# One tile shape for both matmul groups of an attention kernel: 64 rows by 32 columns, with two buffers of scores and two banks of sums

## The chip, the core and the metric

The kernel runs on one core of a Trainium2 chip. A core has five engines that each follow their own instruction queue: TensorE (PE in the profile, with its weight loads shown apart as PEld), VectorE (DVE), ScalarE (ACT), GpSimd (POOL) and SyncE (SP), which here only issues DMAs. Matmul results land in PSUM, which the kernel fills as 8 banks of 128 partitions by 512 fp32 values. The metric is the device time of the whole program in microseconds (us); less is better.

## The reference

Four attention layers, A B A B, on a sequence of 2048 rows of 512 values. Each layer normalises its input, makes 32 query heads of 16 values, but one single key head and one value head that all query heads share, takes a softmax over all 2048 keys, and adds the projected result to its input.

```python
def _A_ref(x, wq, wk, wv, wo):            # H = 32 heads, Dh = 16
    q = (x @ wq).reshape(B, S, H, Dh).transpose(0, 2, 1, 3)
    k = x @ wk                            # one key head for all
    v = x @ wv
    scores = jnp.einsum("bhqd,bkd->bhqk", q, k) * (Dh ** -0.5)
    p = _softmax(scores, axis=-1)
    o = jnp.einsum("bhqk,bkd->bhqd", p, v)
    return o.transpose(0, 2, 1, 3).reshape(B, S, H * Dh) @ wo

x = x + _A_ref(_layernorm(x), A_wq, A_wk, A_wv, A_wo)
x = x + _B_ref(_layernorm(x), B_wq, B_wk, B_wv, B_wo)   # B_ref: the same
x = x + _A_ref(_layernorm(x), A_wq, A_wk, A_wv, A_wo)
x = x + _B_ref(_layernorm(x), B_wq, B_wk, B_wv, B_wo)
```

Every layer computes 32 x 2048 x 2048 scores and as many exponentials.

## The kernel before

**Units.** Queries are handled in blocks of 512 rows (4 per layer) and keys in chunks of 128 (16 per layer). A query block's 32 heads are four groups of eight (`pairs`, 64 of them in all), and a group is worked in two turns of four heads (`odd`). A turn over its chunks is a *segment* (`segs`): 16 chunks, or fewer where the first groups of a layer are cut so that work can start before all keys are there; 156 segments in all. One segment and one chunk make a *unit* (`units`), 2048 in all. A unit has two halves of two heads.

**A step of scores (S).** `scores` (lines 566 to 603) takes one half: two matmuls at line 581 write 128 keys by 512 queries for each of two heads into one tile `st` of 128 x 1024 fp32, which is two PSUM banks. The keys and queries are fp16, each split into a high and a low part, laid out so that one head uses partitions 0 to 63 and the other 64 to 127; the two matmuls are therefore 64 rows by 128 columns of the array and run side by side. Then comes the exponential of the whole tile: on ACT (line 598, one instruction, into a buffer `pt` or `dpt` in SBUF), or, where the order says V, on DVE as a polynomial of seven instructions (`v_exp`, lines 605 to 617), of which only the first, line 609, reads `st`. There are 4096 such halves, 3822 on ACT and 274 on DVE. Where a unit has a half on DVE it is the first one.

**A step of P V (P).** `pv` (lines 619 to 644) takes a finished unit: four fp32 matmuls at line 636, one for each head, multiply the 128 x 32 values (16 value columns and 16 columns of ones, for the numerator and the denominator) with the 128 x 512 exponentials. Each uses all 128 rows and 32 columns of the array, and the four run side by side on the four column groups. They add up into one PSUM bank `acc` over the segment. In the trace each of these fp32 matmuls is two, so a P shows as 8. At the end of a segment `merge` (lines 505 to 519) adds the bank into two SBUF tiles, `num` and `den`, with two DVE instructions (line 515 for the first segment of a group, line 518 for the others); then the quotient is taken in five DVE instructions (lines 537 to 541).

**Background.** Everything else (normalisation, queries, keys, values, the output projection) is cut into small steps by generators; a step (M) often holds three matmuls of 128 x 128 by 512 (lines 297 to 299), sometimes four transposes (line 338), sometimes no matmul.

**PSUM.** `sps` holds NST = 3 buffers of scores of two banks each, `aps` two banks `acc0` and `acc1`. One of these is the sum of the running segment, the other serves the background steps (`bank`); they change roles between segments.

**The order** is written out by hand in a string, ORDER, of 8972 letters, which the loop at lines 673 to 682 follows: S a half with its exponential on ACT, V a half with its exponential on DVE, P, Q, R or T a P step for the first, second, ... unit that waits, M, m or l a background step, v the next instruction of a DVE exponential, d the next instruction of a quotient. The schedule is manual, so each engine gets its instructions in this order, and each works through its own queue in order. A buffer is handed on by semaphores: a step S may write a buffer of scores once the exponential that read it before has ended. Thus PE, in front of an S whose buffer is still being read, waits, and all that stands behind waits with it.

Of the kernel before, what the change touches and what calls it, by code (L numbers as in the profile page):

```python
# [9 lines left out]
F32 = mybir.dt.float32  # L10
# [4 lines left out]
ALU = mybir.AluOpType  # L15
# [4 lines left out]
P = 128  # L20
# [9 lines left out]
NM = H * DH // P  # L30
NK = S // P
W = 2
NST = 3
NPT = 8
EPS = 1e-5
SCALE = DH ** -0.5
# [144 lines left out]
def fast_path(ctx, tc, x_in, weights, out, flag):  # L181
    nc = tc.nc
    PE, V, G, SP = nc.tensor, nc.vector, nc.gpsimd, nc.sync
# [12 lines left out]
    state = dict(idle=0, pool=None, end=False, seg=0)  # L196
# [3 lines left out]
    def bank(name):  # L200
        if state["pool"] is not None:
            return state["pool"].tile([P, 512], F32, name=name, tag="ps")
        if state["end"]:
            return sps.tile([P, W * 512], F32, name="st")[:, :512]
        return aps.tile([P, 512], F32, name=name, tag=f"acc{state['idle']}")


    ident = one.tile([P, P], F32, name="ident")
# [1 line left out]
    half = one.tile([P, 2], F32, name="half")  # L210
# [18 lines left out]
    kop = [[one.tile([P, BQ], F16, name=f"kop{i}_{b}") for b in range(NB)] for i in range(2)]  # L229
# [18 lines left out]
    for i, (_, wk, wv, _) in enumerate(weights):  # L248
        t = one.tile([P, NC, 2, DH], F32, name="wkvl")
# [56 lines left out]
    def load_x(l, b):  # L306
        for t in range(4 * b, 4 * b + 4):
            xt[l, t] = xts.tile([P, D], F32, name="xt")
            SP.dma_start(xt[l, t], x_in[t * P:(t + 1) * P, :] if l == 0 else xscr[t])
# [37 lines left out]
    def keys_values(l, b):  # L347
# [3 lines left out]
        yield False  # L351

        ps = bank("kps")
        for c in range(NC):
            mm3(ps, [w[:, c] for w in wkv[i]], [p[:, c] for p in xT], c == 0, c == NC - 1)
# [66 lines left out]
    def outputs(l, b, ms):  # L422

        yield False
        w = wt["wo", l]
        last = NM - 1 in ms
        for t in range(4 * b, 4 * b + 4):
            ps = bank("ops")
            for k, m in enumerate(ms):
                cols = slice((t - 4 * b) * P, (t - 4 * b + 1) * P)  # L430
                mm3(ps, [p[:, cols] for p in ot[l, b, m]], [p[:, m] for p in w],
                    k == 0, k == len(ms) - 1)
                if k < len(ms) - 1:
                    yield True
            x = xt[l, t]
            V.scalar_tensor_tensor(x, ps, 1 / VS / WS, x, ALU.mult, ALU.add)  # L436
            if last:
                del xt[l, t]
                if l == NL - 1:
                    SP.dma_start(out[t * P:(t + 1) * P, :], x)  # L440
                else:
                    SP.dma_start(xscr[t], x)
                    xt[l + 1, t] = x
            if t < 4 * b + 3:
                yield False
        bg.done.update(("o", l, b, m) for m in ms)
# [50 lines left out]
    qt = {}  # L497
    acc = {}
    sums = {}
    p_of = {}  # L500
    left = {}
# [3 lines left out]
    def merge(s):  # L505


        pr, odd, c0, c1 = segs[s]
        a = acc.pop(s)
        l, b, m = pairs[pr]  # L510
        f = (hi, lo) if odd else (lo, hi)
        if pr not in sums:
            sums[pr] = [one.tile([P, BQ], F32, name=f"{n}{pr % 4}") for n in ("num", "den")]
            for t, k in zip(sums[pr], f):
                V.tensor_scalar(t, a, k, None, ALU.mult)
        else:
            for t, k in zip(sums[pr], f):
                V.scalar_tensor_tensor(t, a, k, t, ALU.mult, ALU.add)  # L518
        if not (odd and c1 == NK):
            return  # L520
        num, den = sums.pop(pr)
        r = one.tile([P, BQ], F32, name="tmp")
        if (l, b) > (0, 0):
            bg.need(("o",) + ((l, b - 1, m) if b else (l - 1, NB - 1, m)))
        last = b == NB - 1

        n = P if last and m == NM - 1 else BQ
        o = []

        def begin():  # L530
            o.extend(one.tile([P, BQ], F16, name=f"ot{m}_{k}") for k in range(2))
            ot[l, b, m] = o

        for c in range(0, BQ, n):
            c = slice(c, c + n)
            div_ops.extend([
                lambda c=c: V.reciprocal(den[:, c], den[:, c]),  # L537
                lambda c=c: V.stream_shuffle(r[:, c], den[:, c], swap),
                lambda c=c: V.tensor_tensor(num[:, c], num[:, c], r[:, c], ALU.mult),
                lambda c=c: (o or begin(), V.tensor_copy(o[0][:, c], num[:, c])),  # L540
                lambda c=c: V.tensor_tensor(o[1][:, c], num[:, c], o[0][:, c], ALU.subtract)])

        def then():
            if m == 1:
                load_x(l, b)
                bg.add(outputs(l, b, [0, 1]))
            elif m == 2 and last:
                bg.add(outputs(l, b, [2]))
            elif m == 3:
                bg.add(outputs(l, b, [3] if last else [2, 3]))  # L550
                if l < NL - 1:
                    bg.add(normed(l + 1, b), keys_values(l + 1, b))
                    if last:
                        bg.add(load_split(("wo", l + 1), weights[(l + 1) % 2][3]))
                        if l == 0:
                            bg.add(ranges(1, "wo"))
                    bg.add_later(queries(l + 1, b))
                    if last and l == NL - 2:
                        bg.add_later(verdict())
                    if last and l < NL - 2:  # L560
                        bg.add_later(load_split(("wq", l + 2), weights[l % 2][0]))

        op = div_ops.pop()
        div_ops.append(lambda: (op(), then()))

    def scores(n, on_v):

        u, half = units[n // 2], n % 2
        s, c = u
        pr, odd, c0, c1 = segs[s]  # L570
        l, b, m = pairs[pr]
        if half == 0:
            if c % 4 == 0:
                bg.need(("k", l, c // 4))
            if s in loads and c == max(c0, c1 - 6):
                qt[segs[s + 1][0]] = load_q(*pairs[segs[s + 1][0]])
        st = sps.tile([P, W * 512], F32, name="st")
        for k in range(W):

            r = slice(64 * k, 64 * k + 64)  # L580
            PE.matmul(st[:, k * 512:(k + 1) * 512],  # L581
                      kop[l % 2][c // 4][r, (c % 4) * P:(c % 4 + 1) * P],
                      qt[pr][r, 2 * half + odd], start=True, stop=True)
        if on_v:
            split.add(u)
        if u in split:
            if half == 0:
                state["dpt"] = dps.tile([P, 2, W * 512], F32, name="dpt")
            pt = state["dpt"][:, half]
        else:  # L590
            pt = pts[:, len(exps) % NPT]
        p_of[u, half] = pt
        if half:
            waiting.append(u)
        if on_v:
            v_exp(pt, st)
            return
        e = nc.scalar.activation(pt, st, AF.Exp, scale=SCALE / UP / UP).ins  # L598
        if u not in split:

            if len(exps) >= NPT:
                tc.declare_no_dep(e, exps[-NPT], reason="behind the reads in between")
            exps.append(e)
# [15 lines left out]
    def pv(k):  # L619

        u = [u for u in waiting if u[0] == state["seg"]][k]
        waiting.remove(u)
        s, c = u
        pr, odd, c0, c1 = segs[s]
        l = pairs[pr][0]
        bg.need(("v", l, c // 4))
        if s not in acc:

            if not bg.open:
                state["idle"] = 1 - state["idle"]  # L630
            acc[s] = aps.tile([P, 512], F32, name="acc", tag=f"acc{1 - state['idle']}")
            left[s] = c1 - c0
        left[s] -= 1
        for j in range(4):
            v = vop4 if u in split and j % 2 == 0 else vop
            PE.matmul(acc[s][32 * j:32 * j + 32, :],  # L636
                      v[l % 2][c // 4][:, c % 4, 16 * odd:16 * odd + 32],
                      p_of[u, j % 2][:, (j // 2) * 512:(j // 2 + 1) * 512],
                      start=left[s] == c1 - c0 - 1, stop=left[s] == 0,
                      skip_group_check=True, tile_position=(0, 32 * j))  # L640
        del p_of[u, 0], p_of[u, 1]
        if left[s] == 0:
            state["seg"] += 1
            merge(s)
# [16 lines left out]
    state.update(pool=None, idle=1)  # L661
    sps = ctx.enter_context(tc.tile_pool(name="sps", bufs=NST, space=PSUM))
    aps = ctx.enter_context(tc.tile_pool(name="aps", bufs=1, space=PSUM))
# [177 lines left out]
```

## Time and profile before

| | before |
|---|---|
| time, median of 2 runs | 3643.06 us (3642.78 to 3643.34) |
| profiled execution, span | 3639.3 us |
| outside the span (median less span) | 3.8 us |
| granted TensorE clock, mean | 0.996 |
| PE busy | 98% of the span, 26707 matmuls |
| ACT busy | 98% |
| DVE busy | 85% |
| POOL busy | 3% |

The span runs from the first to the last instruction of the profiled execution. "Busy" counts an instruction from its start to its end; the ends of matmuls are modelled and neighbours overlap, so a PE at 98% can still be waiting inside. ACT's instructions also overlap a little: one starts before the one ahead has ended. In rows of the timeline the first column is the start in us from the start of the span, the second how long the row's instructions took together, and "x16" says that 16 instructions of the same kind were merged into the row.

### The profile page before, as it was taken

To read this page: it belongs to the slowest core of one execution; us is meant where nothing else is said; L and a number is where in the kernel's file an instruction comes from. 1 tells how busy PE (TensorE), PEld (TensorE's weight loads), DVE (VectorE), ACT (ScalarE), POOL (GpSimd) and SP (SyncE) were. 2 spreads that over 40 slices of the span, in tenths; PEclk is the share of its full clock that TensorE was granted. 3 is DMA by queue.
4 is the path that set the end of the run, shared out by engine and by line. 5 is a ranking of instruction groups with operands and counts; after the bars stand their busy time and mean duration, and the time that the engine had idled before them with its cause. 6 is when DMAs were issued, how large, how long until landed. Compare 5 with 4: busy or idle time off the path is not lost.

```text
span 3639.3 us, 63025 instructions
## 1 busy us (share of the span) xinstructions
PE 3575.5 (98%) x26707; PEld 925.5 (25%) x26707; DVE 3084.4 (85%) x3606; ACT 3552.5 (98%) x3828; POOL 116.8 (3%) x122
## 2 busy tenths in 40 slices
PE   7999999999999999999999999999999999999998
PEld 2222222222222222222222222222222222222221
DVE  4598989998578998988958889988986889899988
ACT  6999999999999999999999999999999999999997
POOL 1000000000000000000000000000000000000000
PEclk9999999999999999999999999999999999999999
DMA  2110100000010010101001000010101101010000
GB/s 89 41 53 13 47 11 29 21 30 30 24 50 21 24 36 13 41 19 36 24 30 45 15 29 25 18 42 18 47 7 36 47 16 36 21 36 13 23 20 13
DMA packets 94819, 108.11 MB, mean 30 GB/s; under 512 B 15936, under 2 KB 72256, under 8 KB 94528
## 3 DMA queue, kind: packets, MB, share of 16 engines
q1 hardware_dynamic: 94208, 102.95, 8.8%
q8 instruction: 211, 3.46, 0.4%
q0 software_dynamic: 320, 1.05, 0.1%
q14 instruction: 80, 0.66, 0.1%
HBM read 70.39 MB, written 33.55 MB: 29 GB/s over the span
## 4 chain that ended last, share of the span: by engine, by line
PE 86%; ACT 11%; DVE 2%; DMA 1%; issue 0%; SPq 0%; POOL 0%; ACTq 0%; DVEq 0%; POOLq 0%
PE acc L636 47%; PE st L581 27%; ACT pt L598 10%; PE qps L297 2%; PE ops L297 2%; PE qps L298 1%; PE qps L299 1%; PE ops L299 1%; PE ops L298 1%; ACT dpt L598 1%; PE tps L338 1%; PE kps L297 0%; DVE den L537 0%; PE kps L299 0%; PE kps L298 0%
## 5 line engine op out<-in xcount | busy, mean ns | idle before, releaser
L598 ACT ACTIVATE pt<-st 128x1024 f32<-128x1024 f32 x3548 | 3311.5, 1046 | 41.0 <-PE st L581 30.4
L636 PE MATMUL acc<-pt,vop 128*32 128x512 f32 x14192 | 1799.5, 601 | 0.1
L581 PE MATMUL st<-qt,kop 64*128 64x512 f16 x8192 | 1269.5, 382 | 30.8 <-DMA qt<-qs 9.7
L581 PEld LDWEIGHTS <-kop 64*128 64x128 f16 x8192 | 357.0, 94 | 1581.5 <-issue 1474.1
L636 PEld LDWEIGHTS acc<-pt,vop 128*32 128x32 f32 x14192 | 345.5, 108 | 704.8 <-issue 684.7
L609 DVE TENSOR_SCALAR e<-st 128x1024 int32<-128x1024 f32 x274 | 335.3, 1224 | 199.3 <-PE st L581 194.8
L617 DVE SCALAR_TENSOR_TENSOR dpt<-dpt,e 128x1024 f32<-128x1024 f32 x274 | 339.7, 1240 | 8.5
L615 DVE SCALAR_TENSOR_TENSOR dpt<-dpt,mant 128x1024 f32<-128x1024 f32 x274 | 338.9, 1237 | 7.1
L616 DVE SCALAR_TENSOR_TENSOR dpt<-dpt,mant 128x1024 f32<-128x1024 f32 x274 | 336.9, 1230 | 7.6
L614 DVE SCALAR_TENSOR_TENSOR dpt<-mant 128x1024 f32<-128x1024 f32 x274 | 336.4, 1228 | 0.0
L636 PE MATMUL acc<-dpt,vop 128*32 128x512 f32 x2192 | 290.8, 602 | 0.0
L598 ACT ACTIVATE dpt<-st 128x1024 f32<-128x1024 f32 x274 | 282.9, 1033 | 5.0 <-ACT pt L598 4.3
L537 DVE RECIPROCAL den<-den 128x512 f32<-128x512 f32 (+1 forms) x76 | 215.9, 2841 | 0.4
L613 DVE TENSOR_SCALAR e<-e 128x1024 int32<-128x1024 int32 x274 | 193.6, 707 | 7.9
L611 DVE TENSOR_SCALAR mant<-e 128x1024 int32<-128x1024 int32 x274 | 189.8, 693 | 8.2
L436 DVE SCALAR_TENSOR_TENSOR xt<-ops,xt 128x512 f32<-128x512 f32 x140 | 96.4, 688 | 79.0 <-PE ops L299 78.1
L403 POOL TENSOR_TENSOR sq<-qs 128x512 bf16<-128x512 f16 x64 | 66.8, 1043 | 1611.6 <-DVE qs L400 1611.6
L518 DVE SCALAR_TENSOR_TENSOR num<-acc,half,num 128x512 f32<-128x512 f32 x92 | 69.0, 750 | 56.6 <-PE acc L636 55.7
L297 PE MATMUL ops<-wo,ot 128*128 128x512 f16 x252 | 97.4, 386 | 3.7 <-DVE xt L436 3.7
L297 PE MATMUL qps<-xnT,wq 128*128 128x512 f16 x256 | 99.1, 387 | 1.4 <-DVE wq L269 0.7
L298 PE MATMUL qps<-xnT,wq 128*128 128x512 f16 x256 | 97.4, 380 | 0.6 <-DVE xnT L342 0.6
L299 PE MATMUL qps<-xnT,wq 128*128 128x512 f16 x256 | 97.3, 380 | 0.4 <-DVE wq L270 0.4
(99 smaller groups left out, 1383.2 us busy)
## 6 DMA issues: line engine op xcount, KB each, us to landing
qt<-qs SPq DMA_DIRECT2D x624, 64.0 KB, 2.2
qs<-qs SPq DMA_DIRECT2D x64, 256.0 KB, 2.2
xs<-xt SPq DMA_DIRECT2D x48, 256.0 KB, 2.0
xt<-xs SPq DMA_DIRECT2D x48, 256.0 KB, 3.4
xt<-in_A_x_dram SPq DMA_DIRECT2D x32, 256.0 KB, 3.5
out_dram<-xt SPq DMA_DIRECT2D x16, 256.0 KB, 2.1
wst<-in_A_wo_dram SPq DMA_DIRECT2D x8, 256.0 KB, 2.7
wst<-in_B_wq_dram SPq DMA_DIRECT2D x8, 256.0 KB, 2.7
```

The source lines that it names most:

```text
L297: PE.matmul(ps, a[0], b[0], start=first, stop=False)
L537: lambda c=c: V.reciprocal(den[:, c], den[:, c]),
L581: PE.matmul(st[:, k * 512:(k + 1) * 512], kop[l % 2][c // 4][r, (c % 4) * P:(c % 4 + 1) * P], qt[pr][r, 2 * half + odd], start=True, stop= ...
L598: e = nc.scalar.activation(pt, st, AF.Exp, scale=SCALE / UP / UP).ins
L609: V.tensor_scalar(e, st, SCALE / UP / UP * LOG2E * 2.0 ** 23, 127 * 2.0 ** 23, ALU.mult, ALU.add)
L611: lambda: V.tensor_scalar(mant.bitcast(I32), e, 0x7FFFFF, 0x3F800000, ALU.bitwise_and, ALU.bitwise_or),
L613: lambda: V.tensor_scalar(e, e, 0x7F800000, None, ALU.bitwise_and),
L614: lambda: V.scalar_tensor_tensor(p, mant, C3, mant, ALU.add, ALU.mult),
L615: lambda: V.scalar_tensor_tensor(p, p, C2, mant, ALU.add, ALU.mult),
L616: lambda: V.scalar_tensor_tensor(p, p, C1, mant, ALU.add, ALU.mult),
L617: lambda: V.scalar_tensor_tensor(p, p, C0, e.bitcast(F32), ALU.add, ALU.mult)])
L636: PE.matmul(acc[s][32 * j:32 * j + 32, :], v[l % 2][c // 4][:, c % 4, 16 * odd:16 * odd + 32], p_of[u, j % 2][:, (j // 2) * 512:(j // 2 + ...
```

## The change

Both groups of matmuls take the same tile of the array, 64 rows by 32 columns, of which eight fit side by side.

A step S becomes eight matmuls instead of two: for each of the two heads four, one for each 32 keys of the chunk. They write the same two banks.

A step P becomes eight fp32 matmuls instead of four: each head's is cut into keys 0 to 63 and keys 64 to 127. The two row halves of the array write two different banks of sums, `acc..0` and `acc..1`, and `merge` adds up both, with two DVE instructions for each.

The sums now take four banks (two for each of the two roles), so the scores are left with four: NST goes from 3 to 2. Background steps use the first bank of the idle pair. ORDER is unchanged.

```diff
-NST = 3
+NST = 2
@@ bank
-        return aps.tile([P, 512], F32, name=name, tag=f"acc{state['idle']}")
+        return aps.tile([P, 512], F32, name=name, tag=f"acc{state['idle']}0")
@@ merge
             for t, k in zip(sums[pr], f):
-                V.tensor_scalar(t, a, k, None, ALU.mult)
-        else:
+                V.tensor_scalar(t, a[0], k, None, ALU.mult)
+            a = a[1:]
+        for x in a:
             for t, k in zip(sums[pr], f):
-                V.scalar_tensor_tensor(t, a, k, t, ALU.mult, ALU.add)
+                V.scalar_tensor_tensor(t, x, k, t, ALU.mult, ALU.add)
@@ scores
-            PE.matmul(st[:, k * 512:(k + 1) * 512],
-                      kop[l % 2][c // 4][r, (c % 4) * P:(c % 4 + 1) * P],
-                      qt[pr][r, 2 * half + odd], start=True, stop=True)
+            for j in range(4):
+                n0 = (c % 4) * P + 32 * j
+                PE.matmul(st[32 * j:32 * j + 32, k * 512:(k + 1) * 512],
+                          kop[l % 2][c // 4][r, n0:n0 + 32], qt[pr][r, 2 * half + odd],
+                          start=True, stop=True, tile_position=(64 * k, 32 * j))
@@ pv
-            acc[s] = aps.tile([P, 512], F32, name="acc", tag=f"acc{1 - state['idle']}")
+            i = 1 - state["idle"]
+            acc[s] = [aps.tile([P, 512], F32, name=f"acc{k}", tag=f"acc{i}{k}") for k in range(2)]
...
-            PE.matmul(acc[s][32 * j:32 * j + 32, :],
-                      v[l % 2][c // 4][:, c % 4, 16 * odd:16 * odd + 32],
-                      p_of[u, j % 2][:, (j // 2) * 512:(j // 2 + 1) * 512],
-                      start=left[s] == c1 - c0 - 1, stop=left[s] == 0,
-                      skip_group_check=True, tile_position=(0, 32 * j))
+            for k in range(2):
+                r = slice(64 * k, 64 * k + 64)
+                PE.matmul(acc[s][k][32 * j:32 * j + 32, :],
+                          v[l % 2][c // 4][r, c % 4, 16 * odd:16 * odd + 32],
+                          p_of[u, j % 2][r, (j // 2) * 512:(j // 2 + 1) * 512],
+                          start=left[s] == c1 - c0 - 1, stop=left[s] == 0,
+                          skip_group_check=True, tile_position=(64 * k, 32 * j))
```

## The prediction

> **What bounds the kernel now.** I read the page first: the busy line, the chain that ended last, and the costliest groups.
>
> ```profile
> span 3639.3 us, 63025 instructions
> ...
> PE 3575.5 (98%) x26707; PEld 925.5 (25%) x26707; DVE 3084.4 (85%) x3606; ACT 3552.5 (98%) x3828; POOL 116.8 (3%) x122
> ...
> PE 86%; ACT 11%; DVE 2%; DMA 1%; issue 0%; SPq 0%; POOL 0%; ACTq 0%; DVEq 0%; POOLq 0%
> ...
> L598 ACT ACTIVATE pt<-st 128x1024 f32<-128x1024 f32 x3548 | 3311.5, 1046 | 41.0 <-PE st L581 30.4
> L609 DVE TENSOR_SCALAR e<-st 128x1024 int32<-128x1024 f32 x274 | 335.3, 1224 | 199.3 <-PE st L581 194.8
> ```
>
> The chain names PE, but PE and ACT are both busy for 98%, so neither number says which has slack. For ACT that can be read from the spacing of its exponentials, where nothing comes between them, and from the first and last start:
>
> ```profile
> 2496.84 15.69 ACT L598 ACTIVATE pt<-st 128x1024 f32<-128x1024 f32 x17
> 2512.23 1.22 ACT L598 ACTIVATE dpt<-st 128x1024 f32<-128x1024 f32 x1
> ```
>
> ```profile
> L598 ACT ACTIVATE pt<-st x3548: 1012/1036/1203, 36.1 to 3618.1; 128x1024 f32<-128x1024 f32 x198
> L598 ACT ACTIVATE dpt<-st x274: 1017/1024/1216, 182.5 to 3610.8; 128x1024 f32<-128x1024 f32 x137
> ```
>
> Seventeen exponentials start in 2512.23 - 2496.84 = 15.39 us: one per **0.905 us**, though each lasts 1.036. That is ACT's own pace. 3548 + 274 = 3822 of them need 36.1 + 3821 x 0.905 + (3639.3 - 3618.1) = **3515 us**; this is the floor that the change doesn't touch, and the kernel stands only 124 us above it. Whatever PE gains, no more than these 124 us (3.4%) can come of it.
>
> Next, PE's own prices, from the timeline of PE:
>
> ```profile
> 2020.12 1.92 PE L636 MATMUL acc<-pt,vop 128*32 128x512 f32 x16
> 2021.98 0.82 PE L581 MATMUL st<-qt,kop 64*128 64x512 f16 x6
> 2022.73 1.92 PE L636 MATMUL acc<-pt,vop 128*32 128x512 f32 x16
> 2024.59 0.60 PE L581 MATMUL st<-qt,kop 64*128 64x512 f16 x4
> 2025.12 1.07 PE L636 MATMUL acc<-dpt,vop 128*32 128x512 f32 x8
> 2026.12 0.60 PE L581 MATMUL st<-qt,kop 64*128 64x512 f16 x4
> ...
> 2030.30 0.39 PE L581 MATMUL st<-qt,kop 64*128 64x512 f16 x2
> 2030.62 0.39 PE L297 MATMUL ops<-wo,ot 128*128 128x512 f16 x1
> ...
> 2031.38 0.61 PE L581 MATMUL st<-qt,kop 64*128 64x512 f16 x4
> ```
>
> From start to start: three S take 0.75, two 0.53, one 0.32. So an S is **0.215** and there is 0.10 more where the kind changes. Two P take 1.86, one 1.00: a P is **0.86**, and a change back to S is 0.14. A background triple takes 0.76 to the next S: 0.65 and 0.11.
>
> Last, the two delays of a buffer's round trip. ACT's end to the S that waited for it:
>
> ```profile
> 2014.80 1.02 ACT L598 ACTIVATE dpt<-st 128x1024 f32<-128x1024 f32 x1
> ```
>
> ```profile
> 2015.87 0.39 PE L581 MATMUL st<-qt,kop 64*128 64x512 f16 x2
> ```
>
> 14.80 + 1.02 = 15.82, and S starts at 15.87: **0.05**. And S to the exponential that waited for it:
>
> ```profile
> 307.43 1.07 ACT L598 ACTIVATE dpt<-st 128x1024 f32<-128x1024 f32 x1
> ...
> 308.19 0.82 PE L581 MATMUL st<-qt,kop 64*128 64x512 f16 x6
> ...
> 308.62 1.02 ACT L598 ACTIVATE pt<-st 128x1024 f32<-128x1024 f32 x1
> ```
>
> At its own pace ACT would have started at 308.34; it started 308.62 - 308.19 = **0.43** after the S.
>
> **The change, part by part.** *One tile shape.* It takes away the change of kind between S and P, if the shape is what costs it. Two things with one shape and different types stand next to each other in the trace:
>
> ```profile
> 68.61 0.40 PE L414 MATMUL gps<-sq,bones 128*32 128x512 bf16 x4
> ...
> 68.84 0.38 PE L416 MATMUL gps<-ksq,bones 128*32 128x512 bf16 x1
> 68.84 1.03 PE L636 MATMUL acc<-pt,vop 128*32 128x512 f32 x7
> ```
>
> bf16 and fp32, both 128*32, start together with no 0.10 between. So it is the shape. ORDER has 1451 blocks of P between S; at 0.10 + 0.14 each, some 350 us leave PE's queue. Background steps keep their 0.1.
>
> *More instructions.* An S has 8 pairs of load and matmul instead of 2, a P 16 instead of 8. The trace has no eight tiles. From below: each of them streams the same 512 columns beside the others, so S stays 0.215 and P 0.86. From above: nothing in the trace sustains more than the 4 instructions per 0.215 of an S; fed at that rate, 16 would take 0.86 and a P's 32 1.72, or 4096 x 0.86 + 2048 x 1.72 = 7.0 ms. The nearest row is a P's own start:
>
> ```profile
> 2009.65 0.16 PEld L636 LDWEIGHTS acc<-pt,vop 128*32 128x32 f32 x8 [0.23 <-issue]
> ```
>
> ```profile
> L636 PEld LDWEIGHTS acc<-pt,vop 128*32 128x32 f32 x14192 | 345.5, 108 | 704.8 <-issue 684.7
> ```
>
> Eight loads of 0.11 begin and end within 0.16, so their starts lie within 0.05, 7 ns apart. At that, eight tiles start within 0.05. I keep 0.215 and 0.86, and add 0.025 to the 0.43, since the last tile starts later.
>
> *Two buffers.* This is what decides. Let A be the start of an exponential. With two buffers the S after next may start at A + 1.036 + 0.05 = A + 1.086, and its exponential at A + 1.086 + 0.455 = **A + 1.541**. ACT wants it at A + 1.810. So 0.27 is left, and that is all the room PE has: if an S started as soon as its buffer was free, the next S must start within 0.905 + 0.27 = 1.174 of it, or ACT stands still. Take off the S itself: **0.958** of other work fits between two S. With three buffers it was 0.905 more, and the order was laid out with that.
>
> What lies between neighbouring S in ORDER (V counted as S, v and d left out): nothing 2232 times, P 693, PP 568, M 264, MM 159, PM or MP 109, P and P with an M 49, MMM or MMMM 16, a few others 7. Not each M has a triple: 804 letters, and
>
> ```profile
> L297 PE MATMUL qps<-xnT,wq x256: 377/389/634, 18.3 to 3147.6; 128*128 128x512 f16 x128
> ...
> L297 PE MATMUL ops<-wo,ot x252: 376/389/390, 274.9 to 3588.5; 128*128 128x512 f16 x126
> ...
> L297 PE MATMUL kps<-xnT,wkv x64: 378/389/390, 18.5 to 2785.6; 128*128 128x512 f16 x64
> ```
>
> 256 + 252 + 64 = 572 triples: 0.71 of them. A lone P (0.86) or M (0.85 with its two changes) fits. The others are short by:
> - PP: 1.716 - 0.958 = 0.758; x 568 = 430 us
> - P with M: 0.86 + 0.85 - 0.958 = 0.75; x 109 x 0.71 = 58
> - MM: 1.30 + 0.19 - 0.958 = 0.53; x 159 x 0.71 x 0.71 = 42
> - P, P and M, and the others: 0.758 + 0.71 x 0.85 = 1.36; x 56 = 76
> - MMM: 1.18 x 16 x 0.36 = 7
>
> Together **613 us** of ACT standing still. The full price holds where the S ahead had waited for its buffer. In an unbroken run S S P P S S P P it hadn't: the second S waits 0.08, and the cycle is 0.215 + 0.08 + 0.215 + 1.716 = 2.23 against 1.81, 0.42 per PP: 568 x 0.42 = 239 at the lower end. ORDER mixes these with S S S; I take the full price, since what PE falls behind is caught up only where it would have waited.
>
> *The halves on DVE.* A V takes one of the two buffers and ACT skips it. The S behind it still waits for the exponential ahead of the V, so the next exponential comes at A + 1.541 where ACT is free at A + 0.905: 0.636 x 274 = **174 us**. With three buffers a third tile covers this. Line 609 itself (1.22) ends in time for the buffer after.
>
> *Merge.* Two more DVE instructions per segment:
>
> ```profile
> L518 DVE SCALAR_TENSOR_TENSOR num<-acc,half,num x92: 740/751/753, 57.6 to 3620.4; 128x512 f32<-128x512 f32 x92
> ...
> L515 DVE TENSOR_SCALAR num<-acc,half x64: 650/751/753, 46.3 to 3595.7; 128x512 f32<-128x512 f32 x64
> ```
>
> Two for each of 92 + 64 = 156 segments, some 0.75 each: 156 x 2 x 0.75 = 234 us on DVE, 3084 to 3318. In a span over 4000 that is hidden; DVE waits for `st` before line 609 as it is (194.8 us above). If it weren't, 1.5 us late for a V that follows a merge would move ACT by as much, at most 234 us. I take nothing.
>
> *Sum.* 3515 + 613 + 174 = 4302, and of the present 124 us above the floor I leave a quarter, 30, for the starts of layers and waits for DMAs: a span of 4332. The median stands 3.8 above the profiled span: **4336 us**, 19% slower.
>
> **Rivals.**
> - *Faster: ACT is fed all the same.* PE's 350 us are freed, and S comes early enough if a gap between two S seldom exceeds 0.958; then the time falls to the floor, 3515 to 3560. It decides at that gap: for it speaks that 3189 of 4096 gaps are empty, a P or an M; against it that PP alone is one gap in seven, each 0.758 over, and S can't run ahead on two buffers.
> - *The runs of PP are cheap.* PP at 0.42, the P and M mixtures at half, the rest of the 124 at half: 3515 + 239 + 92 + 174 + 62 = 4082.
> - *Eight tiles don't run as one.* If an S went as two sets of four, 0.43, every one of the some 790 short gaps would lose 0.215 in S and 0.215 in the delay, 340 us, V 59, and lone P up to 0.3 each: 4650 to 4900. The start row of P speaks against it, though it shows four tiles and a filled queue. The Trainium skill, "TensorE: Matmul & The Clock Gate", in its Part 1, has a rule for such a case: with the hardware decoder off, the sequencer spends about 62 ns per matmul, which binds once the array work is shorter than that. By it, as an estimate, eight matmuls would take 0.50 and a P's sixteen 0.99, and PE alone would need 4096 x 0.50 + 2048 x 0.99 + 572 x 0.65 = 4450 us before any wait. The 7 ns of the row are of four tiles already queued, so no run here shows which holds for a long stream.
> - *The change of kind stays* (between fp16 and fp32): 0.24 more per short gap, 790 x 0.24 = 190, and a lone P no longer fits, 693 x 0.14 = 97: 4620. The rows at 68.84 speak against it.
>
> The same skill's "TensorEngine Tiling (Array Packing)", "Restrictions and Gotchas", warns that row tiles press on PSUM because each row tile needs a bank of its own. This change pays that: the second bank of sums is what the third buffer gives way to.
>
> **How the numbers follow.** The forecast 0.72, with its own range of 4150 to 4500; PP cheap 0.10; eight tiles slower 0.08; change of kind stays 0.05; faster 0.04, and 0.01 for no change. A range of 4080 to 4620 takes in the first two and the last but one. 2% (73 us) is about what a measurement of this kernel can tell from no change: faster 0.04, same 0.01, slower 0.95.
>
> **What would show it.** In the profile after: S to S still 0.215 and P 0.86, with no 0.1 at S to P; ACT near 82% busy, its idle time ended by PE's `st`, and its spacing 1.54 behind a V; DVE near 3320 us busy; PE sitting before line 584 for ACT's release. The forecast is wrong if S itself lasts longer, if the exponential is released or fed faster than 0.05 and 0.43, or if PE is behind ACT throughout, so that buffers no longer matter.

## The result, and the profile after

| | before | after |
|---|---|---|
| time, median | 3643.06 us | 4384.35 us (4384.13 to 4384.58) |
| ratio | | 1.2034, 95% interval 1.1999 to 1.2069 |
| profiled span | 3639.3 us | 4382.8 us |
| PE, ACT, DVE busy | 98%, 98%, 85% | 81%, 83%, 75% |

The change makes the kernel 20% slower. The page of the changed kernel, its busy line and its costliest groups:

```profile
span 4382.8 us, 145387 instructions
...
PE 3536.2 (81%) x67667; PEld 1304.7 (30%) x67667; DVE 3299.6 (75%) x3918; ACT 3653.8 (83%) x3828; POOL 116.6 (3%) x122
...
L601 ACT ACTIVATE pt<-st 128x1024 f32<-128x1024 f32 x3548 | 3373.1, 1030 | 511.8 <-PE st L584 508.0
L584 PE MATMUL st<-qt,kop 64*32 64x512 f16 x32768 | 1544.9, 381 | 812.4 <-ACT pt L601 712.1
...
L612 DVE TENSOR_SCALAR e<-st 128x1024 int32<-128x1024 f32 x274 | 335.3, 1224 | 444.7 <-PE st L584 442.3
```

No engine is busy throughout any more. ACT waits for PE (508 us, 30 before) and PE waits for ACT (712 us at line 584), by turns. That is how a loop through too few buffers looks: neither side bounds, the round trip does; the first experiment below shows that it is the buffers. (ACT's idle figure is smaller than what it lost, since an instruction's time covers its tail beyond the 0.905 pace; the loss is counted below from start to start.)

One stretch shows each price. PE and ACT of the changed kernel, from their timelines (start, time together, what, how many; in brackets the idle time before and what ended it):

```profile
2499.92 1.91 PE L642 MATMUL acc<-pt,vop 64*32 64x512 f32 x32
2501.64 0.63 PE L584 MATMUL st<-qt,kop 64*32 64x512 f16 x16
2503.19 0.41 PE L584 MATMUL st<-qt,kop 64*32 64x512 f16 x8 [0.93 <-ACT pt L601]
2503.41 1.48 PE L642 MATMUL acc<-pt,vop 64*32 64x512 f32 x24
```

```profile
2498.64 2.85 ACT L601 ACTIVATE pt<-st 128x1024 f32<-128x1024 f32 x3
2502.12 2.85 ACT L601 ACTIVATE pt<-st 128x1024 f32<-128x1024 f32 x3 [0.63 <-PE st L584]
```

Two P go from 2499.92 to the S at 2501.64 in 1.72, where before the change they took 1.86: the changes of kind are gone on both sides, for the P behind the S at 2503.19 also starts 0.22 later instead of 0.32. So PE's own work became cheaper, as meant. But the S behind the two P came too late: ACT stood idle until 2502.12, 0.48 after that S. Then PE in turn had nothing to do until 2503.19, because both buffers were full.

And a half on DVE:

```profile
2009.34 1.03 ACT L601 ACTIVATE pt<-st 128x1024 f32<-128x1024 f32 x1
2011.00 1.02 ACT L601 ACTIVATE pt<-st 128x1024 f32<-128x1024 f32 x1 [0.63 <-PE st L584]
2012.60 1.03 ACT L601 ACTIVATE dpt<-st 128x1024 f32<-128x1024 f32 x1 [0.58 <-PE st L584]
```

```profile
2010.52 0.63 PE L584 MATMUL st<-qt,kop 64*32 64x512 f16 x16
2011.22 1.23 DVE L612 TENSOR_SCALAR e<-st 128x1024 int32<-128x1024 f32 x1 [1.24 <-PE st L584]
2012.07 0.41 PE L584 MATMUL st<-qt,kop 64*32 64x512 f16 x8 [0.93 <-ACT pt L601]
```

Of the two S from 2010.52 the second is a V, and DVE's line 612 starts at 2011.22. ACT has nothing until the S at 2012.07, which waited for 2011.00 + 1.02 = 2012.02; so two exponentials stand 1.60 apart, where 0.905 would do.

Now the whole trace. For each exponential on ACT I took its start, less the start of the one before, less 0.904, and added this up by what ORDER has between its S and the S ahead; where the S ahead was a V, it stands in the row "behind a V" instead. In the table M stands for any background letter, and "others too" in the last row takes in the lone M and a few rare mixtures. In us, with counts:

```
between the S     count   before   after   two buffers alone   with a buffer for V
P P                 560     53.6   422.8         526.2               527.7
M M                 151     13.9    76.4          62.0                57.3
P and M             105      6.0    38.8          45.9                43.1
P, P and M           49      5.4    33.2          43.6                43.7
M M M                13      3.3    18.3          17.5                17.5
a lone P            611     15.6    33.2          95.3                44.4
nothing            1830     11.4    26.1          21.8                14.9
behind a V (all)    274    14.2   207.7         209.1                33.5
all, others too    3821    127.8   869.4        1032.1               791.5
```

After the change the sum is 869. With 36 us to the first exponential, 3821 x 0.904 = 3454 and 23 us from the start of the last one to the end, that is the span, 4383. This holds by construction: the table shares the time out, and why a gap is long is for the experiments to show. The last two columns are of two of them.

One thing the rows hide. Of the 33 us at a lone P, 26 stand at the 177 of the 611 that come one S further behind a V, and 11 of the 26 us of "nothing" at 35 such places. What a V costs doesn't end with the next exponential; by these rows it comes to some 245 us.

### The profile page after: what moved, and what is told of

Read it like the earlier page. It is cut to its first block, busy times and chain, and to the rows that moved or that the text cites. A ratio compares the mean times of both kernels' runs of the same rounds, so it can differ in the third digit from the quotient of the medians.

```text
span 4382.8 us, 145387 instructions
## 1 busy us (share of the span) xinstructions
PE 3536.2 (81%) x67667; PEld 1304.7 (30%) x67667; DVE 3299.6 (75%) x3918; ACT 3653.8 (83%) x3828; POOL 116.6 (3%) x122
## 5 line engine op out<-in xcount | busy, mean ns | idle before, releaser
L601 ACT ACTIVATE pt<-st 128x1024 f32<-128x1024 f32 x3548 | 3373.1, 1030 | 511.8 <-PE st L584 508.0
L584 PE MATMUL st<-qt,kop 64*32 64x512 f16 x32768 | 1544.9, 381 | 812.4 <-ACT pt L601 712.1
L642 PE MATMUL acc<-pt,vop 64*32 64x512 f32 x28384 | 1795.5, 590 | 0.1
L584 PEld LDWEIGHTS <-kop 64*32 64x32 f16 x32768 | 613.6, 90 | 2317.0 <-issue 2260.6
L642 PEld LDWEIGHTS acc<-pt,vop 64*32 64x32 f32 x28384 | 528.4, 106 | 391.7 <-issue 321.3
L642 PE MATMUL acc<-dpt,vop 64*32 64x512 f32 x4384 | 288.5, 589 | 0.6 <-DVE dpt L620 0.6
L519 DVE SCALAR_TENSOR_TENSOR num<-acc,half,num 128x512 f32<-128x512 f32 x248 | 184.6, 744 | 113.5 <-PE acc L642 113.3
L519 DVE SCALAR_TENSOR_TENSOR den<-acc,half,den 128x512 f32<-128x512 f32 x248 | 184.0, 742 | 0.0
L400 DVE TENSOR_SCALAR qs<-qps 128x512 f16<-128x512 f32 x64 | 43.9, 686 | 89.6 <-PE qps L299 67.7
L297 PE MATMUL qps<-xnT,wq 128*128 128x512 f16 x256 | 99.5, 389 | 1.2 <-ACT xnT L293 0.7
```

The costliest lines, as they stand in the source:

```text
L297: PE.matmul(ps, a[0], b[0], start=first, stop=False)
L519: V.scalar_tensor_tensor(t, x, k, t, ALU.mult, ALU.add)
L584: PE.matmul(st[32 * j:32 * j + 32, k * 512:(k + 1) * 512], kop[l % 2][c // 4][r, n0:n0 + 32], qt[pr][r, 2 * half + odd], start=True, stop= ...
L642: PE.matmul(acc[s][k][32 * j:32 * j + 32, :], v[l % 2][c // 4][r, c % 4, 16 * odd:16 * odd + 32], p_of[u, j % 2][r, (j // 2) * 512:(j // 2 ...
```

## The experiments

**Two buffers and nothing else.** The kernel before, with the tiles as they were:

```diff
-NST = 3
+NST = 2
```

> The kernel before with NST = 2 and nothing else changed (the two PSUM banks that this frees stay unused). Theory (two buffers starve ACT wherever more work lies between two S than the round trip of a buffer leaves room for): slower by more than the whole change, since the change of kind between S and P stays: at a delay of 0.43 a gap may hold 0.984 us; PP is 1.716 + 0.24, short by 0.97 x 568 = 551; a lone P is 1.10, short by 0.114 x 693 = 79; P with M 64, MM 41, P P and M 81, MMM 7; V 0.611 x 274 = 167; 3515 + 990 + 30 = 4535, range 4400 to 4640. Rival (the cost of the change lies in the eight tiles or in the second bank of sums, not in the buffers): 3640 to 3700.

Measured 4546.07 us; the theory gave 4535. Two buffers alone cost 902 us, more than the whole change; the column "two buffers alone" above has its large rows where "after" has them, each larger still where a P, with its changes of kind, lies between. Its page has the same two-sided wait:

```profile
L598 ACT ACTIVATE pt<-st 128x1024 f32<-128x1024 f32 x3548 | 3383.3, 1027 | 662.4 <-PE st L581 661.5
...
L581 PE MATMUL st<-qt,kop 64*128 64x512 f16 x8192 | 1434.6, 382 | 764.1 <-ACT pt L598 681.3
```

Thus the one tile shape, together with its second bank of sums, is a gain of 4546 - 4384 = 162 us where two buffers are given.

**The eight tiles of S alone.** Three buffers, P as it was:

```diff
-            PE.matmul(st[:, k * 512:(k + 1) * 512],
-                      kop[l % 2][c // 4][r, (c % 4) * P:(c % 4 + 1) * P], ...)
+            for j in range(4):
+                n0 = (c % 4) * P + 32 * j
+                PE.matmul(st[32 * j:32 * j + 32, k * 512:(k + 1) * 512],
+                          kop[l % 2][c // 4][r, n0:n0 + 32], ..., tile_position=(64 * k, 32 * j))
```

> The kernel before with only the matmuls of S cut into eight tiles of 64 rows by 32 columns; P stays at 128 x 32 and three buffers stay. Theory: eight tiles cost no more than two (0.216 from S to S), the exponential follows 0.48 after the S instead of 0.43, the change of kind stays at some 0.1; 3640 to 3670. Rival (many small matmuls are what costs): 0.43 for an S puts PE's queue at over 4000, so the time goes above 3900.

Measured 3681.77 us, ratio 1.0103 (1.0086 to 1.0120): 38 us over the kernel before and 12 over the range. The rival, with over 3900, falls: an S stays at 0.216 to the next S. But eight tiles aren't quite free. From an S to the P behind it the median is 0.330, against 0.310 before, and the exponential follows 0.481 after the start of its S, against 0.431. With PE as near to its bound as it is there, 0.02 in each of some 1400 places would be 28 of the 38 us; this is an estimate, and the later exponential may have its part.

**One tile shape with three buffers.** PSUM has no room for three buffers of scores and four banks of sums, so P leaves out half the keys, and with them the second bank:

```diff
-                      v[l % 2][c // 4][:, c % 4, 16 * odd:16 * odd + 32],
-                      p_of[u, j % 2][:, (j // 2) * 512:(j // 2 + 1) * 512],
+                      v[l % 2][c // 4][0:64, c % 4, 16 * odd:16 * odd + 32],
+                      p_of[u, j % 2][0:64, (j // 2) * 512:(j // 2 + 1) * 512],
```

> S in eight tiles and P in tiles of the same 64 x 32 shape, but with three buffers of scores and one bank of sums: to make room, P leaves out keys 64 to 127 of each chunk (four tiles at the place of eight, which last as long). Theory: with one tile shape PE loses the 350 us of changes, and with three buffers ACT is fed nearly throughout: 3540 to 3600, at least 40 below the kernel before. Rival (it is the shape that costs): near 4384.

> One tile shape with three buffers and half of P V again (keys 64 to 127 of each chunk left out), timed in rounds, since a single time 17 us under before can't be told from none. Theory: ACT's pace and the shape's gain put it under the kernel before, but by less than the 350 us that leave PE's queue: 3600 to 3630, ratio 0.988 to 0.996. Rival (the shape gains nothing once ACT bounds): 3644.

Measured 3627.08 in a single run, then 3621.78 us in six (3608.13 to 3634.32), ratio 0.9943 (0.9921 to 0.9964). The shape isn't what costs: with a third buffer it is slightly faster than the kernel before. The first expectation, at least 40 us of gain, was too high. One reason is in the windows of the first run (after the stretch and its length: PE, PEld, DVE, ACT and POOL busy, PE clock, DMA share, GB/s):

```profile
100.00:200.00 100.00, 91.86 (x1118) 33.26 (x1106) 47.16 (x96) 79.71 (x86) 5.13 (x5) 0.81 0.13 38
200.00:300.00 100.00, 98.11 (x1273) 35.45 (x1265) 81.74 (x91) 89.21 (x96) 4.16 (x4) 0.83 0.15 46
300.00:400.00 100.00, 96.58 (x1453) 37.48 (x1446) 89.26 (x94) 99.30 (x109) 3.13 (x3) 1.00 0.08 23
```

In the 200 us where the granted clock was 0.81 and 0.83, ACT lost 36 us between exponentials, against 11 in the same stretch of the kernel before; from 300 us on it lost 69 against 109. In the profiled one of the six runs, where less of that stretch was at a lower clock, it lost 17 and then 70. So this kernel is some 40 us faster at the full clock, a third of the 124 above the floor. Not all of it need be the shape: P's matmuls use one row half here, and S was seen to start on the other half beside them (last section).

**The same half of P with two buffers.**

```diff
-NST = 3
+NST = 2
```

> The same half P V and one bank of sums, with two buffers of scores. Against the changed kernel it lacks the other row half of P, the second bank and the two more DVE instructions per segment. Theory: none of these is on the path, only the buffers: 4340 to 4390. Rival (the merges, some 234 us of DVE, or the other four tiles hold PE up): 4150 or less.

Measured 4496.34 us, above the range. The rival, 4150, falls. The clock was lower here, 0.953 in the mean and, in its windows,

```profile
100.00:200.00 100.00, 87.21 (x944) 30.23 (x940) 42.72 (x84) 69.28 (x74) 4.09 (x4) 0.74 0.13 38
200.00:300.00 100.00, 86.14 (x948) 28.68 (x940) 52.12 (x67) 68.93 (x73) 3.12 (x3) 0.73 0.10 27
```

The trace still tells what the rest is worth. It records the clock as full or half, stretch by stretch. In 3418 of the 3821 steps from one exponential to the next it is full in this run and in the changed kernel's, throughout the step and the 8 us ahead of it. These steps take 3839.0 us here and 3857.1 in the changed kernel. So the second bank, the additional merges and the other row half of P cost the changed kernel some 18 us together there, 0.5%, and the 112 us that this run is longer lie in the other steps, at the lower clock. With two buffers the kernel stays near 4384, with three the same P is near 3627.

**Another order of P.** The changed kernel, with the second of two P behind the next S:

```diff
-    "mSSSMMMSSSPPSSMSSPPSSMMSSSPPSSMMSSPSSPPSSSPPSSMMSSS...
+    "mSSSMMMSSSPSPSMSSPSPSMMSSSPSPSMMSSPSSPSPSSPSPSMMSSS...
```

> The changed kernel with another ORDER: where two P lie between two S, the second is moved behind the next S (its place among the other letters otherwise as it was). Gaps with two P and no M fall from 568 to 72, those with P and M from 109 to 48, P P and M to 6; a lone P rises from 693 to 1841. Same instructions, same counts. Theory (a gap of over 0.95 us between two S is what stops ACT): the shortage falls to 72 x 0.78 + 48 x 0.75 x 0.71 + 161 x 0.53 x 0.5 + 6 x 1.36 + 7 = 140 us; 3515 + 140 + 181 + 30 = 3866, range 3800 to 3960. Rival (PE is behind ACT throughout, or DVE is what holds): within 60 of 4384.

Measured 4133.56 us: 251 less, so the place of P does decide and PE isn't behind throughout, but not the 518 less that I had expected, and above the range. Sorted in the same way, the gaps with two P fell from 423 to 52 us, the expected 56. The gaps add up to 617 us: V 207, M M 96, and 1644 lone P held ACT up for 176 us, against 33 before the move. I had left out three things there. 80 of the 176 stand behind another gap that isn't empty: an S and a P take 0.215 + 0.86 = 1.07, longer than ACT's 0.905, and behind each other they add up. 53 stand one S further behind a V. And 31 stand at 18 of the 20 P that the moved letters bring behind an exponential which writes their buffer `pt` again; such a P reads the later values and waits for them. The changed kernel has no such P. Its page had 0.1 us of waiting at line 642, this one has

```profile
L642 PE MATMUL acc<-pt,vop 64*32 64x512 f32 x28384 | 1887.3, 592 | 29.7 <-ACT pt L601 23.7
```

**The same order with three buffers.** A control: the kernel before with that ORDER.

> The kernel before with the ORDER of the spread run: a control for whether that order is better by itself. Theory: with three buffers a gap with two P was covered already, and more and shorter blocks of P mean more changes of kind (some 500 blocks more at 0.24): 3640 to 3780, not faster. Rival (the order is better whatever the buffers): under 3600.

Measured 3817.77 us, 174 more than with its own order and 38 above the range. It has 1971 blocks of P instead of 1451, each with two changes of kind: 520 x 0.24 = 125 us of PE's time, where PE was at 98%. It also has the 20 P of the run above that wait for a later exponential, and ACT stands still for 44 us right behind these. So with three buffers this order isn't the better one, with or without the 44 us, and the 251 us of the run above go with the two buffers. The control has two tile shapes, though; one shape with three buffers and the whole of P doesn't fit.

**The halves on DVE.** Three forms of the changed kernel without them, V written as S and the letters v left out.

```diff
-    ...SMPSmSPPSSVPvSmSSPSPvSSvSmQSQvSQvSSmSQvSVQSSmPvSSv...
+    ...SMPSmSPPSSSPSmSSPSPSSSmQSQSQSSmSQSSQSSmPSS...
```

> The changed kernel with all 4096 exponentials on ACT: each V is an S, the letters v are left out. Theory (a half on DVE takes one of the two buffers and so costs ACT 0.66 us of standing still, of the 0.905 that it saves): slower by 274 x (0.905 - 0.66) = 67: 4410 to 4490. Rival (a half on DVE costs ACT nothing): slower by 274 x 0.905 = 248: 4630.

Measured 4796.39 us, above both. With 8 buffers `pt` this order writes some of them again before their P has read them, for 468 of the 2048 P, and P waits for the later exponential. The page has a wait that the changed kernel doesn't have:

```profile
L626 PE MATMUL acc<-pt,vop 64*32 64x512 f32 x32768 | 2195.3, 604 | 271.4 <-ACT pt L585 270.9
```

So the run doesn't price a V. The next had more buffers, `NPT = 14`:

> The changed kernel with all exponentials on ACT again, now with 14 buffers pt at the place of 8, so that none of them is written again before its P (with 8, and the halves of DVE in the ring too, 804 of the 2048 P in that order come after an overwriting exponential, read that one and so wait for it). Theory (a half on DVE costs ACT most of what it saves): the trace of the changed kernel puts 205 us of ACT's idle time behind a V; 274 x 0.905 - 205 = 43 more, and some more for gaps that the V had let PE catch up in: 4400 to 4500. Rival (a half on DVE costs ACT nothing): 4384 + 248 = 4630.

Measured 4559.22 us, between the two: 192 of the P still come after an overwriting exponential, since Q takes the second unit that waits and the first stays. (The 804 in the expectation above, and the 343 and 804 in the next, are halves out of 4096, not P.) The third takes the oldest unit always (its order is shown against that of the first two):

```diff
-NPT = 8
+NPT = 14
-    ...SmQSQSQSSmSQSSQ...
+    ...SmPSPSPSSmSPSSP...
```

> The changed kernel with all exponentials on ACT, 14 buffers pt, and P always for the unit that has waited longest (Q written as P), so that no P comes after an exponential that overwrites its own: 0 of 2048, against 343 with Q and 14 buffers and 804 with Q and 8. This is the first of the three forms that has the work of the changed kernel and no other wait. Theory (a half on DVE costs ACT most of what it saves): 4384 + 274 x 0.905 - 205 = 4427, and some more where a V let PE catch up: 4400 to 4500. Rival (a half on DVE costs ACT nothing): 4630.

Measured 4396.42 us, just below the theory's range: 12 us more than with 274 halves on DVE, whose exponentials would take ACT 274 x 0.905 = 248. So with two buffers the halves on DVE give back some 236 of the 248 us, in keeping with the 245 that stand behind a V in the table. The 12 us themselves, from a single run, are hardly more than nothing, and P takes its units in another order here. Its groups show 4096 exponentials on ACT; P has no wait to speak of:

```profile
L585 ACT ACTIVATE pt<-st 128x1024 f32<-128x1024 f32 x4096 | 3848.9, 1037 | 497.5 <-PE st L568 495.2
```

**A buffer of their own for the V halves.** The kernel before with two buffers, and the two banks that become free for V alone:

```diff
-NST = 3
+NST = 2
+    vps = ctx.enter_context(tc.tile_pool(name="vps", bufs=1, space=PSUM))
-        st = sps.tile([P, W * 512], F32, name="st")
+        st = (vps if on_v else sps).tile([P, W * 512], F32, name="st")
```

> The kernel before with NST = 2, and a buffer of their own for the scores of the V halves, in the two PSUM banks that NST = 2 frees. ACT keeps two buffers to itself. Theory (a V costs because it holds one of two buffers): of the 210 us that stand behind a V in the trace of two buffers alone, some 30 stay (a gap with a P and the V's own S between is 1.31 against 0.984): 4546 - 180 = 4366, range 4320 to 4430. Rival (a V costs ACT nothing, the idle time behind it would fall elsewhere): 4546.

Measured 4305.94 us, 240 less than with two buffers alone and below the range: what stands behind a V fell from 209 to 34 as expected, and lone P fell from 95 to 44 besides. That was V too: at the 177 lone P one S further behind a V it fell from 66 to 14, and elsewhere it stayed near 30. The idle time of ACT before an exponential into `dpt`, which is always the next one behind a V, shows the same; first two buffers alone, then this run:

```profile
L598 ACT ACTIVATE dpt<-st 128x1024 f32<-128x1024 f32 x274 | 280.8, 1025 | 176.3 <-PE st L581 81.3
L598 ACT ACTIVATE dpt<-st 128x1024 f32<-128x1024 f32 x274 | 280.6, 1024 | 24.2 <-ACT pt L598 10.1
```

The P P row, 527.7, did not move. The two causes are thus separate and each has its price.

## Why the prediction was right

The time, 4384.35 us, lies 48 above the forecast of 4336 and within its range. The mechanism is as forecast: ACT starves through two buffers wherever more than some 0.95 us of work lies between two S, and behind a V. In the rows of the table the 48 are, rounded, V +34, the 30 us for the rest +37, the mixtures -11, P P -7, and -4 in the floor and outside the span. By its steps:

- **The floor, 3515.** Right: ACT kept its pace where it was fed, and the span less the gaps is 3513.
- **The shape removes the change of kind.** Right: S to P takes 0.215 at the median against 0.310, P to S 0.429 against 0.545. It is worth 162 us with two buffers, the second bank included. With three buffers and half of P the gain is some 40, of which not all need be the shape.
- **Eight tiles cost no more than two.** Right for the pace, 0.216 and 0.858 for a P; the added delay was under-sized: 0.05 where I had taken 0.025. It shows behind a V (below). At P P it doesn't show in the sum.
- **PP short by 0.758, 430 us.** Measured 0.755 each in the mean, 422.8 in all. The full price was the right end; the rival of cheap PP (0.42) falls. With the delay of 0.481 the full price would be 0.783; the median is 0.767, and one in twenty costs 0.33 or less, so two small errors cancel here.
- **The mixtures, 183 in all.** Measured 172, which is luck in part. M M took 76 where I had 42 and M M M 18 where I had 7; P and M 39 for 58, P P and M 33 for most of 76. The wrong step was to take each M as holding a triple in 0.71 of the cases, wherever it stands. In the trace 149 of the 151 gaps M M hold two triples and all 13 M M M three; of the 105 gaps with P and M 13 hold a triple, 44 four other matmuls (mostly transposes) and 46 none; and in none of the 49 with two P does the M hold a matmul.
- **V, 174.** This is the term that was mis-sized most. Measured 208 at the next exponential and some 37 more one S further on, which the forecast had at nothing. The 0.71 of a V with nothing behind it is 0.636 + 0.025 of delay and 0.045 more at an exponential that writes `dpt`: where ACT waits, these start 0.526 after their S at the median, the others 0.480. That V costs because it holds one of two buffers is shown by the run with a buffer for V.
- **Merge, nothing.** DVE did grow to 3299.6 us (3318 forecast) and to 3918 instructions, 312 more. It costs next to nothing: at the full clock, two buffers and half of P without the second bank and its merges take 18 us less in 3857. And with DVE at 29% busy, in the last run without V, ACT waits as much for PE (495 us, 508 in the changed kernel).
- **The lone P, nothing, and 30 for all the rest.** Measured 33 for the lone P, 26 for empty gaps and 7 for a lone M. Of these 67 us 37 belong to V, as above; without them the 30 are right. The lone P in a row, which I had left out, mattered little here and more in the spread order.

The rivals: ACT fed all the same (3515 to 3560) fails on the 878 gaps of the first five rows of the table (two P, or an M beside something else), which hold 590 of the 869 us, and on V. Eight tiles not running as one (4650 to 4900), and with it the estimate of 0.50 for eight matmuls by the Trainium skill's "TensorE: Matmul & The Clock Gate", Part 1, where the sequencer takes 62 ns for each: not what happens here, 0.216. The change of kind that stays (4620): not so. What the Trainium skill's "TensorEngine Tiling (Array Packing)" says under "Restrictions and Gotchas", that row tiles press on PSUM, is what this case turns on: the bank that the second row half needs took the third buffer, and two buffers alone cost 902 us.

## What to carry to other kernels

When PSUM must be shared out again, count the room that a buffer gives before counting what the engine saves: the round trip (read 1.036, release 0.05, refill and delivery 0.48) against as many paces of the consumer as there are buffers, and then every stretch of the producer's order that is longer than what remains. A written order embodies the buffers for which it was written; it can be priced for fewer by counting the letters between two refills. Two engines that wait for each other by turns at some 80% each, where both were at 98%, were the sign of a round trip that is too long here, and work handed to a third engine was worth little where it took a buffer out of that loop. When an order is moved about, see too whether a buffer is written again before its reader has come.

## What was not expected of the hardware

- Eight tiles of 64 x 32 start and run as one, but their exponential follows 0.481 us after the start of S, against 0.431 for two tiles of 64 x 128, in the kernels that have them with whole P and alike with two and with three buffers. From the first to the last of the eight the starts lie 0.024 apart at the median, against 0.003 for the two; the rest is not explained.
- The clock record has two values, full and half. The means of 0.81 and 0.83 (three buffers, 100 to 300 us) and of 0.74 and 0.73 (two buffers) in the kernels whose P uses half of the rows are mixtures of both: in the first, half from 107 to 131 and from 186 to 234 us. Such a kernel spent 113 us (three buffers), 69 (the same kernel again) and 420 (two buffers) at half clock, the changed kernel 42. But the first run without V, with whole P, spent 171, so the idle rows alone don't explain it, and their part wasn't tried.
- With P on one row half, S starts on the other half without waiting: from the last pass of a P to the first matmul of the next S the median is some 0.31 in the run with three buffers and half of P, where the changed kernel has 0.429, the length of a pass. In that run's timeline four of the eight matmuls of an S start before the last four of the P ahead, although the program issues that P first, and the other four only at 2004.33; in 2196 of the 4096 S only four start together.

```profile
2002.61 1.46 PE L638 MATMUL acc<-pt,vop 64*32 64x512 f32 x12
2003.52 0.40 PE L583 MATMUL st<-qt,kop 64*32 64x512 f16 x4
2003.90 0.60 PE L638 MATMUL acc<-pt,vop 64*32 64x512 f32 x4
2004.33 0.60 PE L583 MATMUL st<-qt,kop 64*32 64x512 f16 x12
```
